# Scores of a half head scaled, masked and minimised by two whole-tile instructions in place of one accumulating instruction per block

## The chip, the cores and the metric

The kernel runs on one core of a Trainium2 chip. The metric is the device time of one execution in microseconds. Three runs of the kernel before gave 688.06, 691.05 and 696.49 us. The engines are TensorE (PE, with its weight loads as PEld), VectorE (DVE), ScalarE (ACT), GpSimd (POOL) and SyncE (SP, which issues DMAs).

## What is computed

Three layers follow each other on 4 sequences of 576 tokens. The change lies in the first.

```python
scores = scale * q @ k.T                 # 4 x 8 heads, 576 x 576, head_dim 64, scale 1/8
rel = pos[:, None] - pos[None, :]
mask_plain = (rel >= 0) & (rel < 32)                       # heads 0 to 3
mask_dil = (rel >= 0) & (rel < 128) & (rel % 4 == 0)       # heads 4 to 7
scores = where(mask, scores, -1e9)
attn = exp(scores - max(scores)); attn /= sum(attn) + 1e-9
x = attn @ v
```

The second layer routes each token to one of 8 experts (relu(x w1[e]) w2[e], times a probability) by a gate that can keep the expert of the token before; the third is a gated unit with a spatial product over the 576 tokens (relu(x w_in), normalised half, mixed over tokens, gate, w_out).

## The kernel before, in words

**Attention** (`attention`, line 583) goes through 64 half heads: 16 pairs of heads (4 sequences x 4 pairs), each with two halves and two heads. A sequence's pairs 0 and 1 are "plain" heads: a half is 3 blocks of 96 queries against 128 keys. Pairs 2 and 3 are dilated heads, handled by residue modulo 4: a half is 4 blocks of 72 queries against 72 keys (first half) or 104 keys (second half). `geom` (line 722) gives these sizes. So 32 half heads have 3 blocks of 96x128, 16 have 4 of 72x72 and 16 have 4 of 72x104; in their order, 8 plain half heads are followed by 8 dilated ones (72, 72, 104, 104 columns and again).

One half head i passes these steps: `qk` (line 727) multiplies queries and keys into a PSUM tile `S` of [128, 4, 128] (two buffers); `soft` (line 743) on VectorE computes, block by block, (score + mask) x -0.125 into `ms` and the minimum of each row into `mxa` (line 751, one accumulating instruction a block), and POOL then subtracts the minimum (line 754); `expo` (line 759) takes exp(-ms) on ScalarE; `pT` (line 767) transposes on TensorE and evacuates to `ptS`; `pv` (line 778) multiplies with the values on TensorE into a PSUM tile `PV` (two buffers, line 787), then adds 1e-9 to the sums (line 793), takes the reciprocal (line 795) and writes `xo`, the product of both (line 797), the last three on VectorE. Every second half head a finished part of x is transposed, split into a high part `xTh` on ScalarE and a low part `xTl` on VectorE (lines 550 and 551), for the router.

**The order** of every engine's instructions is the order in which the program writes them. The loop at line 877 writes, in turn i: `qk(i)`, `soft(i)`, then what is left of `fill` and of the router's budget, one transposition of later queries or keys, `expo(i-1)`, `pT(i-3)`, the product of `pv(i-4)`, and a transposition of x. The three VectorE steps of `pv` are put between the instructions of `soft` of the next turn: `advance()` writes the next of them, and `feed(i)` writes one step of the router (a small VectorE, ScalarE or PE instruction), while the turn's budget lasts (10 or 5 steps). In the kernel before, `advance()` and `feed(i)` are called behind each block, 3 or 4 times a half head.

`evac` (line 639) sends an evacuation to ScalarE or VectorE, whichever has less in `load_of`; `soft` adds a figure to both at lines 756 and 757. The masks are made at lines 584 to 588 by POOL: `masks[:, 0]` for a first block, `masks[:, 1]` for the others; the fill `MASKED` is added before the scaling, hence -8e9.

After attention come the expert blocks, whose first products begin while attention ends, and the third layer.

Of the kernel before, what the change touches and what calls it, by code (L numbers as in the profile page):

```python
# [10 lines left out]
F32 = mybir.dt.float32  # L11
# [5 lines left out]
ALU = mybir.AluOpType  # L17
AX = mybir.AxisListType
# [43 lines left out]
PTL = 3  # L62
QB, KB = 96, 128
QD, KD = 72, 104
MASKED = -8.0e9
GATE = -1.5 * 2.0 ** -23


# [1 line left out]
def moe_stack(ctx: ExitStack, tc: tile.TileContext, q, k, v, w_gate, w_local, w1, w2, w_in, w_sp, b_sp, w_out, out):  # L70
    nc = tc.nc
# [63 lines left out]
    def steps(f):  # L135

        g = f()
        if g is not None:
            yield from g
# [441 lines left out]
    load_of = {"act": 0.0, "dve": 0.0}  # L581

    def attention(aw, ap, qkp, plan):
        masks = aw.tile([QB, 2, KB], F32, name="masks", bufs=1)
        nc.gpsimd.memset(masks, 0.0)
        for m in range(2):
            for base, cm, st in ((32 * m, 1, -1), (31 - 32 * m, -1, 1)):
                nc.gpsimd.affine_select(out=masks[:, m], in_=masks[:, m], pattern=[[st, KB]], compare_op=ALU.is_ge, fill=MASKED, base=base, channel_multiplier=cm)
        loads, qT, xout = {}, {}, {}
        xTs = {}  # L590

# [130 lines left out]
        def geom(u, half):  # L722
            if u % 4 < 2:
                return QB, KB, 3
            return QD, (QD, KD)[half], 4
# [17 lines left out]
        def soft(i):  # L743
            u, hh, half = hs[i]
            nq, nk, nb = geom(u, half)
            ps = live[i][0]
            ms = aw.tile([96, 4, 128], F32, name="ms", bufs=2)
            mx = aw.tile([96, 4], F32, name="mxa", bufs=3)
            for j in range(nb):
                m = 0 if (half == 0 and (u % 4 >= 2 or j == 0)) else 1  # L750
                nc.vector.tensor_tensor_reduce(out=ms[0:nq, j, 0:nk], in0=ps[0:nq, j, 0:nk], in1=masks[0:nq, m, 0:nk], scale=-0.125, scalar=3.0e38, op0=ALU.add, op1=ALU.min, accum_out=mx[0:nq, j:j + 1])  # L751
                advance()
                feed(i)
            nc.gpsimd.tensor_tensor(out=ms[0:nq, 0:nb, 0:nk], in0=ms[0:nq, 0:nb, 0:nk], in1=mx[0:nq, 0:nb].unsqueeze(2).to_broadcast([nq, nb, nk]), op=ALU.subtract)  # L754
            live[i] += [ms, mx]
            load_of["dve"] += 520 + nb * (70 + nk * 1.04)
            load_of["act"] += 190 + nb * nk * 0.84

        def expo(i):
# [76 lines left out]
        def advance():  # L836
            for _ in range(len(fill)):
                g = fill.popleft()
                if next(g, fill) is not fill:
                    fill.append(g)  # L840
# [6 lines left out]
        name, ends = [None, None], {}  # L847

        def feed(i):

            nonlocal budget
            for n in FIRST:
                while budget > 0:
                    if begun[n] is None:
                        if not queues[n]:
                            break
                        f = queues[n][0]
                        if hasattr(f, "on_pe") and i < ends.get(getattr(f, "needs", None), ended[n]) + GAP:
                            break
                        begun[n], name[n] = steps(queues[n].popleft()), f  # L860
                    cost = next(begun[n], fill)
                    if cost is fill:
                        begun[n], ended[n], ends[name[n]] = None, i, i
                        continue
                    budget -= cost or 1
                    load_of["dve"] += STAGE_COST * (cost or 1)
                    return
# [9 lines left out]
        for i in range(n_hs + LAG + EXTRA):  # L877
# [4 lines left out]
            if i < n_hs:  # L882
                u, hh, half = hs[i]
                if i % 4 == 3 and u >= EU or i % 4 == 0 and u <= EU:
                    w = u + 2 if i % 4 else u + 1
                    if w < npair:
                        urgent.extend(turns(w))
                if i % 4 == 3:
                    if u + 4 < npair:
                        load_qk(u + 4)  # L890
                    if 3 <= u + 2 < npair:
                        load_v(u + 2)
                qk(i)
                if i < 6:
                    heat(HS[i])
                soft(i)
# [11 lines left out]
            if 0 <= i - LAG < n_hs:  # L908
                fill.append(pv(i - LAG))
                advance()  # L910
                u, hh, half = hs[i - LAG]
# [27 lines left out]
    aw = aws.enter_context(tc.tile_pool(name="aw", bufs=2))  # L939
# [166 lines left out]
    ready = {"w1": lambda: state["listed"] > 1, "in": lambda: "idx1" in state}  # L1106
    plan = [(i, ready.get(kind, lambda: True), early(kind, c)) for i, kind, c in PLAN]
    stages = attention(aw, ap, qkp, plan)
    done = {"gather": 2, 1: 2, 2: 2}

# [382 lines left out]
```

## Time and profile before

| what | value |
|---|---|
| median of three runs | 691.05 us |
| the profiled execution | 691.2 us |
| its span, first to last instruction | 689.5 us |
| PE busy | 665.4 us, 97% |
| PEld busy | 572.5 us, 83% |
| DVE busy | 420.9 us, 61% |
| ACT busy | 378.0 us, 55% |
| POOL busy | 122.8 us, 18% |

Busy time of an engine is the time in which at least one of its instructions runs; instructions of one engine can overlap, so that their durations add up to more. "Idle before" is the engine's idle time ahead of an instruction, with what ended it; a wait for several things is put down to the last. Times in a timeline count from the first instruction.

### The profile page before, as it was taken

The numbers are of one execution on the slowest core, as the hardware profiler recorded it, in microseconds if no ns is written. First come the engines' busy times: TensorE is split into PE (matmuls) and PEld (weight loads), VectorE is DVE, ScalarE is ACT, GpSimd is POOL, SyncE is SP. The second block draws the span as 40 slices with busy tenths as digits, with TensorE's granted clock in tenths as the row PEclk, the third lists the DMA queues.
The fourth block names the chain that finished last, engine by engine and source line by source line (L and its number), as shares of the span: only waits on it lengthen the run. The fifth ranks groups of instructions, "written<-read, shape, count | busy, mean of one in ns | idle before, by whom it ended". The sixth has DMA issues, their size and how long they took to land. (4 is left out here: it accounts for less than half of the span.)

```text
span 689.5 us, 14119 instructions
## 1 busy us (share of the span) xinstructions
PE 665.4 (97%) x4393; PEld 572.5 (83%) x4394; DVE 420.9 (61%) x1411; ACT 378.0 (55%) x780; POOL 122.8 (18%) x194
## 2 busy tenths in 40 slices
PE   8899898989999999999999999988999999999998
PEld 6899898886478888888888887867998998998996
DVE  4577969878866747978876856333764164064051
ACT  5688676763635746767665647435725327235322
POOL 6343424441212101101111031002100110000000
PEclk9999999999999999999999999999999999999999
DMA  8876555595445876786565755415100210200102
GB/s 153 173 174 156 120 132 142 148 340 171 154 152 182 299 245 200 284 318 202 221 215 207 290 175 223 154 48 165 47 17 31 68 41 0 77 17 1 61 2 76
DMA packets 98321, 101.34 MB, mean 147 GB/s; under 512 B 59200, under 2 KB 68672, under 8 KB 98240
## 3 DMA queue, kind: packets, MB, share of 16 engines
q1 hardware_dynamic: 94800, 89.10, 42.0%
q0 software_dynamic: 3440, 11.27, 5.0%
q8 instruction: 36, 0.59, 0.3%
q14 instruction: 45, 0.37, 0.2%
HBM read 139.68 MB, written 17.30 MB: 228 GB/s over the span
## 5 line engine op out<-in xcount | busy, mean ns | idle before, releaser
L1045 PE MATMUL yp<-w2h,hh 128*128 128x512 f32 x176 | 70.9, 403 | 0.5 <-ACT hh L1034 0.5
L982 POOL DMA_INDIRECT xs<-x_d,ix x25 | 30.6, 1225 | 225.7 <-DVE ix L980 67.9
L1047 PE MATMUL yp<-w2h,hl 128*128 128x512 f32 x176 | 69.0, 392 | 0.8 <-DVE hl L1035 0.8
L1046 PE MATMUL yp<-w2l,hh 128*128 128x512 f32 x176 | 68.5, 389 | 0.0
L1011 PE MATMUL hp<-w1h,xh 128*128 128x512 f32 x168 | 67.5, 401 | 0.2 <-issue 0.2
L1013 PE MATMUL hp<-w1h,xl 128*128 128x512 f32 x168 | 65.8, 392 | 0.1
L1012 PE MATMUL hp<-w1l,xh 128*128 128x512 f32 x168 | 65.6, 391 | 0.0
L751 DVE CUSTOM_DVE_ANT_0 ms<-S,masks 96x128 f32<-96x128 f32 (+2 forms) x224 | 54.5, 249 | 18.0 <-PE S L740 9.5
L754 POOL TENSOR_TENSOR ms<-ms,mxa 96x384 f32<-96x384 f32 (+2 forms) x64 | 51.1, 798 | 67.2 <-DVE mxa L751 39.4
L551 DVE TENSOR_TENSOR w2l<-raw,w2h 128x1024 fp32r<-128x1024 f32 x40 | 47.7, 1223 | 14.8 <-ACT w2h L550 13.1
L740 PE MATMUL S<-kz,qT 128*96 128x128 f32 (+2 forms) x448 | 54.0, 262 | 0.2 <-POOL kz L602 0.2
L787 PE MATMUL PV<-vt,ptS 128*96 128x65 f32 (+2 forms) x448 | 44.9, 242 | 7.0 <-issue 2.3
L1035 DVE TENSOR_TENSOR hl<-hTp,hh 128x512 fp32r<-128x512 f32 x44 | 30.4, 690 | 33.7 <-ACT hh L1034 33.2
L551 DVE TENSOR_TENSOR w1l<-raw,w1h 128x1024 fp32r<-128x1024 f32 x40 | 46.4, 1223 | 4.1 <-ACT w1h L550 3.3
L787 PEld LDWEIGHTS PV<-vt,ptS 128*96 128x96 f32 (+2 forms) x448 | 39.3, 158 | 9.5 <-issue 3.2
L740 PEld LDWEIGHTS S<-kz,qT 128*72 128x72 f32 (+1 forms) x448 | 46.1, 158 | 0.9 <-POOL kz L602 0.7
L550 ACT ACTIVATE w2h<-raw 128x1024 fp32r<-128x1024 f32 x40 | 41.2, 1060 | 5.0 <-PE yp L1047 3.8
L550 ACT ACTIVATE gtiles<-gt 128x288 fp32r<-128x288 f32 (+2 forms) x48 | 15.7, 359 | 48.3 <-DVE gt L1389 48.3
L1034 ACT ACTIVATE hh<-hTp 128x512 fp32r<-128x512 f32 x44 | 26.2, 596 | 28.4 <-DVE hl L1035 22.9
L1047 PEld LDWEIGHTS yp<-w2h,hl 128*128 128x128 f32 x176 | 33.0, 188 | 9.0 <-DVE hl L1035 1.9
L550 ACT ACTIVATE w1h<-raw 128x1024 fp32r<-128x1024 f32 x40 | 39.3, 1048 | 2.1 <-ACT w1h L550 0.9
L765 ACT ACTIVATE pp<-ms 96x384 f32<-96x384 f32 (+2 forms) x64 | 32.2, 504 | 12.0 <-POOL ms L754 11.4
(310 smaller groups left out, 1725.1 us busy)
## 6 DMA issues: line engine op xcount, KB each, us to landing
raw<-in_moe_w SPq DMA_DIRECT2D x188, 512.0 KB
y_d<-y SPq DMA_DIRECT2D x30, 256.0 KB
qk<-in_q SPq DMA_DIRECT2D x32, 144.0 KB
qk<-in_k SPq DMA_DIRECT2D x32, 144.0 KB
x_d<-xo SPq DMA_DIRECT2D x32, 144.0 KB
scratch<-in_moe_w_in SPq DMA_DIRECT2D x8, 512.0 KB
out<-o SPq DMA_DIRECT2D x15, 256.0 KB
vt<-in_v SPq DMA_DIRECT2D x48, 64.0 KB
```

What stands on the lines that cost most here:

```text
L550: nc.scalar.activation(dst_h, src, AF.Copy)
L551: (eng or nc.vector).tensor_tensor(out=dst_l, in0=src, in1=dst_h.bitcast(F32), op=ALU.subtract)
L740: nc.tensor.matmul(ps[0:nq, j, 0:nk], l, r, start=True, stop=True)
L751: nc.vector.tensor_tensor_reduce(out=ms[0:nq, j, 0:nk], in0=ps[0:nq, j, 0:nk], in1=masks[0:nq, m, 0:nk], scale=-0.125, scalar=3.0e38, op0= ...
L754: nc.gpsimd.tensor_tensor(out=ms[0:nq, 0:nb, 0:nk], in0=ms[0:nq, 0:nb, 0:nk], in1=mx[0:nq, 0:nb].unsqueeze(2).to_broadcast([nq, nb, nk]), ...
L787: nc.tensor.matmul(ops[0:nq, j], ptS[0:nk, j, 0:nq], r, start=True, stop=True)
L1011: nc.tensor.matmul(ps[n], xh[:, kk], wh[:, kk, cs], start=(kk == 0), stop=False)
L1012: nc.tensor.matmul(ps[n], xh[:, kk], wl[:, kk, cs], start=False, stop=False)
L1013: nc.tensor.matmul(ps[n], xl[:, kk], wh[:, kk, cs], start=False, stop=(kk == 3))
L1045: nc.tensor.matmul(ps, hh[:, f], P["w2h"][:, f], start=(f == 0), stop=False)
L1046: nc.tensor.matmul(ps, hh[:, f], P["w2l"][:, f], start=False, stop=False)
L1047: nc.tensor.matmul(ps, hl[:, f], P["w2h"][:, f], start=False, stop=(f == 7))
```

## The change

The mask tile has four planes (the last two are copies of the second), its fill is 1e9, added after the scaling. Per half head, one scalar_tensor_tensor over all 3 or 4 blocks computes score x -0.125 + mask, and one tensor_reduce takes the minimum of each block's rows. Two calls each of `advance()` and `feed(i)` lie between the two and two behind them, 4 in every half head. The load figure for VectorE is another.

```diff
@@ -62,7 +62,7 @@
 PTL = 3
 QB, KB = 96, 128
 QD, KD = 72, 104
-MASKED = -8.0e9
+MASKED = 1.0e9
 GATE = -1.5 * 2.0 ** -23
 
 
@@ -581,11 +581,12 @@
     load_of = {"act": 0.0, "dve": 0.0}
 
     def attention(aw, ap, qkp, plan):
-        masks = aw.tile([QB, 2, KB], F32, name="masks", bufs=1)
-        nc.gpsimd.memset(masks, 0.0)
+        masks = aw.tile([QB, 4, KB], F32, name="masks", bufs=1)
+        nc.gpsimd.memset(masks[:, 0:2], 0.0)
         for m in range(2):
             for base, cm, st in ((32 * m, 1, -1), (31 - 32 * m, -1, 1)):
                 nc.gpsimd.affine_select(out=masks[:, m], in_=masks[:, m], pattern=[[st, KB]], compare_op=ALU.is_ge, fill=MASKED, base=base, channel_multiplier=cm)
+        nc.vector.tensor_copy(masks[:, 2:4], masks[:, 1:2].to_broadcast([QB, 2, KB]))
         loads, qT, xout = {}, {}, {}
         xTs = {}
 
@@ -746,14 +747,23 @@
             ps = live[i][0]
             ms = aw.tile([96, 4, 128], F32, name="ms", bufs=2)
             mx = aw.tile([96, 4], F32, name="mxa", bufs=3)
-            for j in range(nb):
-                m = 0 if (half == 0 and (u % 4 >= 2 or j == 0)) else 1
-                nc.vector.tensor_tensor_reduce(out=ms[0:nq, j, 0:nk], in0=ps[0:nq, j, 0:nk], in1=masks[0:nq, m, 0:nk], scale=-0.125, scalar=3.0e38, op0=ALU.add, op1=ALU.min, accum_out=mx[0:nq, j:j + 1])
-                advance()
-                feed(i)
+            if u % 4 < 2:
+                mk = masks[0:nq, half:half + nb, 0:nk]
+            else:
+                mk = masks[0:nq, half:half + 1, 0:nk].to_broadcast([nq, nb, nk])
+            nc.vector.scalar_tensor_tensor(out=ms[0:nq, 0:nb, 0:nk], in0=ps[0:nq, 0:nb, 0:nk], scalar=-0.125, in1=mk, op0=ALU.mult, op1=ALU.add)
+            advance()
+            feed(i)
+            advance()
+            feed(i)
+            nc.vector.tensor_reduce(mx[0:nq, 0:nb], ms[0:nq, 0:nb, 0:nk], axis=AX.X, op=ALU.min)
+            advance()
+            feed(i)
+            advance()
+            feed(i)
             nc.gpsimd.tensor_tensor(out=ms[0:nq, 0:nb, 0:nk], in0=ms[0:nq, 0:nb, 0:nk], in1=mx[0:nq, 0:nb].unsqueeze(2).to_broadcast([nq, nb, nk]), op=ALU.subtract)
             live[i] += [ms, mx]
-            load_of["dve"] += 520 + nb * (70 + nk * 1.04)
+            load_of["dve"] += 640 + nb * nk * 2.08
             load_of["act"] += 190 + nb * nk * 0.84
 
         def expo(i):
```

## Rows read from the trace of the kernel before

**Rows 1.** Section 1 of the page: busy us (share of the span), instructions.

```profile
PE 665.4 (97%) x4393; PEld 572.5 (83%) x4394; DVE 420.9 (61%) x1411; ACT 378.0 (55%) x780; POOL 122.8 (18%) x194
```

**Rows 2.** Busy time by stretches: from:to, length, engines' busy time (instructions), granted clock, DMA.

```profile
40.40:64.60 24.20, 23.61 (x278) 22.55 (x276) 17.03 (x121) 19.71 (x50) 10.03 (x17) 1.00 0.69 158
64.60:84.40 19.80, 17.13 (x198) 16.06 (x198) 18.40 (x112) 14.46 (x38) 9.17 (x16) 0.96 0.54 130
...
104.20:133.70 29.50, 26.10 (x299) 23.94 (x298) 27.94 (x172) 21.27 (x53) 13.08 (x23) 1.00 0.54 130
...
144.60:156.70 12.10, 10.23 (x106) 9.56 (x104) 10.14 (x67) 6.88 (x17) 4.33 (x7) 0.86 1.05 354
...
200.00:420.00 220.00, 220.00 (x1079) 183.30 (x1078) 156.66 (x237) 135.06 (x195) 29.45 (x32) 1.00 0.68 242
```

**Rows 3.** Waits of PE, 40 to 160 us: us in total, times, longest.

```profile
PE PV L787 <- DVE xo L797: 1.4, 3, 0.8
```

**Rows 4.** Groups by form, line 751, VectorE: count, busy us, mean ns, idle before.

```profile
L751 DVE CUSTOM_DVE_ANT_0 ms<-S,masks 96x128 f32<-96x128 f32 x96 | 25.5, 273 | 7.8 <-PE S L740 4.4 <-ACT pp L765 3.2
...
L751 DVE CUSTOM_DVE_ANT_0 ms<-S,masks 72x104 f32<-72x104 f32 x64 | 15.9, 248 | 3.1 <-PE S L740 3.0
L751 DVE CUSTOM_DVE_ANT_0 ms<-S,masks 72x72 f32<-72x72 f32 x64 | 13.7, 215 | 7.1 <-ACT ls L163 3.9 <-PE S L740 2.1 <-PE R L468 0.9
```

**Rows 5.** Timeline of VectorE, one plain half head: start us, length us.

```profile
43.33 0.28 DVE L751 CUSTOM_DVE_ANT_0 ms<-S,masks 96x128 f32<-96x128 f32 x1
43.54 0.08 DVE L751 DVE_READ_ACCUMULATOR2_ANT mxa<- 96x1 f32 x1
...
43.91 0.25 DVE L751 CUSTOM_DVE_ANT_0 ms<-S,masks 96x128 f32<-96x128 f32 x1
...
44.09 0.41 DVE L797 TENSOR_TENSOR xo<-PV,rc 72x256 f32<-72x256 f32 x1
```

**Rows 6.** Timeline of VectorE, end of a 72x72 half head and a 72x104 one.

```profile
36.41 0.22 DVE L751 CUSTOM_DVE_ANT_0 ms<-S,masks 72x72 f32<-72x72 f32 x1
36.56 0.08 DVE L751 DVE_READ_ACCUMULATOR2_ANT mxa<- 72x1 f32 x1
36.68 0.26 DVE L751 CUSTOM_DVE_ANT_0 ms<-S,masks 72x104 f32<-72x104 f32 x1
36.87 0.08 DVE L751 DVE_READ_ACCUMULATOR2_ANT mxa<- 72x1 f32 x1
...
37.22 0.23 DVE L751 CUSTOM_DVE_ANT_0 ms<-S,masks 72x104 f32<-72x104 f32 x1
...
37.38 0.42 DVE L797 TENSOR_TENSOR xo<-PV,rc 72x256 f32<-72x256 f32 x1
```

**Rows 7.** Timeline of VectorE, three scalar_tensor_tensor; the third reads what the second writes.

```profile
259.40 0.69 DVE L1081 SCALAR_TENSOR_TENSOR scratch<-scratch 128x512 f32<-128x512 uint32 x1
260.01 0.69 DVE L1082 SCALAR_TENSOR_TENSOR scratch<-scratch 128x512 int32<-128x512 int32 x1
260.73 0.69 DVE L1083 SCALAR_TENSOR_TENSOR scratch<-scratch 128x512 f32<-128x512 f32 x1
```

**Rows 8.** Line 487, the widest reduce: ns min/median/max, starts, forms.

```profile
L487 DVE TENSOR_REDUCE pv<-pm x1: 903/903/903, 217.9 to 217.9; 128x90 f32<-128x720 f32 x1
```

**Rows 9.** Timeline, two places: an xo and the second product that follows it.

```profile
32.35 0.35 DVE L797 TENSOR_TENSOR xo<-PV,rc 96x192 f32<-96x192 f32 x1
...
32.85 0.31 PE L787 MATMUL PV<-vt,ptS 72*72 72x65 f32 x2
...
90.75 0.35 DVE L797 TENSOR_TENSOR xo<-PV,rc 96x192 f32<-96x192 f32 x1
...
91.32 0.47 PE L787 MATMUL PV<-vt,ptS 128*96 128x65 f32 x3
```

**Rows 10.** Timeline, start: POOL's masks and VectorE's first copy of scores' operands.

```profile
3.84 1.25 POOL L588 TENSOR_SCALAR_AFFINE_SELECT masks<-masks 96x128 f32<-96x128 f32 x4
...
6.39 0.45 DVE L645 COPY kz<-T 64x288 f32<-64x288 f32 x1 [2.11 <-PE T L670]
```

## The prediction, made before the change was run

> **What bounds the kernel now.** I read the page first: TensorE is busy for 97% of the span and VectorE for 61% [rows 1], so extra VectorE work should cost nothing on the average, and the question is where it is not average. Next I read busy time by stretches, cut at the starts of half heads. Attention, where the edited instructions run, ends near 157 us. In 40.4:64.6 VectorE is busy for 17.03 of 24.20 us and TensorE for 23.61: TensorE sets the pace. In 64.6:84.4, 104.2:133.7 and 144.6:156.7, where the router's small VectorE steps fall, VectorE is busy for 18.40 of 19.80, 27.94 of 29.50 and 10.14 of 12.10 us, and TensorE loses 2.67, 3.40 and 1.87 us. In 200:420 TensorE is busy for all of 220.00 us [rows 2]; so a microsecond lost in attention is not won back there. The waits of TensorE between 40 and 160 us then name what it lacks: the second product (L787) waits on VectorE's `xo` (L797), which frees its PSUM buffer [rows 3]. The chain that ended last covers only the tail of the program and doesn't help.
>
> **What goes.** 64 half heads lose their 224 accumulating instructions, each with an accumulator read, on a form 96x128 (32 half heads of 3), 72x104 (16 of 4) and 72x72 (16 of 4) [rows 4]. Their durations, 273, 248 and 215 ns, are not what they cost: VectorE starts the next instruction before the last has ended. The timeline shows 0.21 us from a 96x128 to what follows (43.33 to 43.54), the second the same, and 0.18 for the third (43.91 to 44.09): 0.60 us a half head [rows 5]. For 72x104 it is 0.19, 0.18, 0.16 and 0.18 (first and third shown), together 0.71 us; for 72x72 0.15, 0.15, 0.12 and 0.15, together 0.57 us [rows 6]. The accumulator read takes no slot of its own: what follows starts at the same moment. So 32 x 0.60 + 16 x 0.71 + 16 x 0.57 = 39.7 us of VectorE's time go.
>
> **What comes.** One scalar_tensor_tensor and one reduce per half head, over 384, 416 or 288 columns. The same kind of scalar_tensor_tensor over 512 columns lets its successor start after 0.61 us (259.40 to 260.01) and lasts 0.69 [rows 7]; at 0.96 GHz 512 columns are 0.533 us, so 0.08 us is fixed: 0.475, 0.51 and 0.375 us. The reduce of 720 columns lasts 903 ns [rows 8], that is 0.153 + 720 x 1.042 ns; with the same 0.08 us of overlap it blocks VectorE for 0.47, 0.50 and 0.37 us. Together 0.945, 1.01 and 0.745 us, and 32 x 0.945 + 16 x 1.01 + 16 x 0.745 = 58.3 us. Difference a half head: +0.345, +0.30, +0.175 us; in all +18.6 us of VectorE. The cause is plain: each column now passes VectorE twice.
>
> [...]
>
> **What moves.** The reciprocal now follows the add that feeds it directly when no router step lies between. A dependent successor starts 0.72 us after an instruction that lasts 0.69 [rows 7], so the add (0.15 us long, 0.07 of slot) holds it to 0.18 us. `xo` then starts 0.475 + 0.18 + 0.09 + 0.47 = 1.215 us after the half head's first instruction instead of 0.76 [rows 5], 0.455 later; 0.58 later for 72x104 (0.70 now [rows 6]) and 0.43 for 72x72 (0.59).
>
> **On the path: the saturated stretches.** 64.6:84.4 holds 3 plain half heads, 3 of 72x104 and 2 of 72x72: 1.04 + 0.90 + 0.35 = 2.3 us more; 104.2:133.7 holds 7, 3 and 2: 3.7 us; 144.6:156.7 holds 0, 3 and 2: 1.25 us. VectorE's idle time there is 1.40, 1.56 and 1.96 us [rows 2]. If it takes up all it can, 0.9 + 2.1 + 0 = 3.0 us reach TensorE; if none, because VectorE idles while it waits for ScalarE and those waits move along, 7.2 us. I take 4.5: part of the idle time is such waiting, and a stretch may hand some lag on to the easier one behind it.
>
> **On the path: elsewhere.** VectorE has room, but `xo` comes later, and in seven places outside those stretches a second product starts at most 0.50 us after the end of `xo`; the first at 32.85 (`xo` ends 32.70), the last at 91.32 (`xo` ends 91.10) [rows 9]. About 0.08 us between the two is the hand-over. Growth by 0.43 to 0.58 us less the margins of 0.02 to 0.42 gives 0.51, 0.13, 0.16, 0.44, 0.28, 0.44 and 0.32: 2.3 us. Zero if a stall at one place gives the next its margin back; I take 1.5.
>
> **At nothing.** The copy of the mask (96x256) waits for POOL's mask, done at 5.09 us, on a VectorE that then stands idle until 6.39 [rows 10]; without that cover it would cost 0.35 us. The scores' bank comes free earlier, but no wait of TensorE is put on it, so no gain. The minimum is complete some 0.3 us later in plain half heads (1.215 + 0.08 behind the first instruction, against 0.58 + 0.25 + 0.08 + hand-over [rows 5]) and about as early as now in the others; the exponential is used two half heads later, which hides it: between -1 and +1 us in all, taken as 0. The raised load figure of line 756 can only move evacuations from VectorE to ScalarE, which spares VectorE a little; also 0.
>
> **Sum.** The profiled execution took 691.2 us (span 689.5): 691.2 + 4.5 + 1.5 = 697.2. The median of the three runs shown, 691.05, is 0.15 lower, so I predict 697.0. A measurement of this kernel tells about 2% (14 us) from no change, so this would be within it.
>
> **Rivals.** Absorbed: TensorE is the bound, S and PV are double-buffered, VectorE's lag is used up in the stretches between; 691 to 692. For it: 23.61 of 24.20 us in 40.4:64.6 [rows 2]. Against it: TensorE's direct waits on `xo`. Chance 0.22.
>
> Faster, because fewer instructions: if VectorE worked them off end to end, a half head would cost 3 x (273 + 80) = 1.06, 4 x (248 + 80) = 1.31 and 4 x (215 + 80) = 1.18 us now [rows 4, 5], and 1.11, 1.18 and 0.91 by the full durations of rows 7 and 8 after: +0.05, -0.13, -0.27. The three stretches would gain 0.8 + 0.5 + 0.9 us, and the time be 689. It decides at whether a successor waits for the accumulator read, and the starts say that it doesn't [rows 5, 6]. Chance 0.06. [...]
>
> [...] Chance 0.12, half of it over 2%.
>
> That the compiler splits the new instructions back into blocks, and the time stays: 0.02.
>
> **How the numbers follow.** Forecast (694 to 701) 0.58. The range 690 to 703 leaves out most of the gain and the far end of the clock case. Slower by over 2%: 0.06 of the clock case and 0.01 else, 0.07; faster by over 2% would need more than half of all TensorE's idle time, 0.02; within 2%: 0.91.
>
> **What would show it.** Right: 64 scalar_tensor_tensor near 560, 593 and 460 ns and 64 reduces near 553, 587 and 454; VectorE's busy time up by some 15 us; `xo` 1.1 to 1.3 us behind its half head's first instruction; longer waits of L787 on L797; TensorE busier by nothing and idle longer in the three stretches. Wrong: a reduce well under 400 ns, unchanged waits on `xo`, or a shorter time to the start of the first expert block.

## The result and the profile after

The changed kernel took 698.86 us (median of 4 runs, 698.29 to 701.07), the kernel before 690.63 in the same comparison (4 runs, 688.06 to 696.49): a ratio of 1.0125, 95% interval 1.0094 to 1.0157, slower by some 8 us. In a second comparison (9 runs against 19) it took 697.61 against 690.63: 1.0097, 1.0062 to 1.0131. The profiled execution shown here is the longest of the first four, 701.07 us, so the single trace overstates the difference. The profiled execution of the kernel before took 691.2 us.

Section 1 of the page of the changed kernel, for [rows 1]:

```profile
PE 670.8 (96%) x4393; PEld 575.9 (82%) x4394; DVE 440.5 (63%) x1088; ACT 380.0 (54%) x784; POOL 123.5 (18%) x194
```

VectorE has 323 instructions fewer and is busy 19.6 us longer (440.5 - 420.9). The fewer instructions do more work.

Busy time by stretches of the changed kernel, with the columns of [rows 2]. The first six follow each other and are cut at the same half heads as the rows of before; the last lies in the expert blocks:

```profile
41.40:67.50 26.10, 24.08 (x277) 22.77 (x277) 20.53 (x71) 19.98 (x51) 9.76 (x17) 1.00 0.62 141
67.50:88.80 21.30, 17.59 (x196) 15.81 (x195) 20.82 (x69) 14.25 (x37) 9.33 (x16) 0.96 0.52 121
88.80:111.80 23.00, 22.63 (x210) 21.33 (x209) 15.29 (x55) 14.20 (x37) 6.67 (x14) 0.82 0.49 110
111.80:143.70 31.90, 26.02 (x296) 23.75 (x295) 31.13 (x115) 21.28 (x53) 13.04 (x23) 1.00 0.50 126
143.70:154.80 11.10, 11.10 (x127) 10.11 (x127) 8.64 (x37) 7.43 (x22) 5.03 (x10) 1.00 1.02 298
154.80:167.00 12.20, 9.74 (x96) 9.12 (x94) 10.92 (x34) 6.76 (x16) 4.30 (x6) 0.86 1.04 378
210.00:430.00 220.00, 220.00 (x1079) 183.25 (x1078) 156.96 (x237) 135.23 (x195) 30.24 (x32) 1.00 0.69 242
```

The third and the fifth of these stretches were, in the kernel before:

```profile
84.40:104.20 19.80, 19.47 (x207) 18.30 (x207) 12.47 (x94) 13.80 (x37) 6.74 (x13) 0.95 0.58 130
...
133.70:144.60 10.90, 10.79 (x124) 9.81 (x123) 6.88 (x58) 7.49 (x22) 5.06 (x10) 1.00 0.97 305
```

Compare the lengths, the first number behind each window, with [rows 2] and these two. Up to the first cut 1.0 us is added (41.4 for 40.4), then 1.9, 1.5, 3.2, 2.4, 0.2 and 0.1 us: 10.3, against 9.8 between the two spans (699.3 - 689.5). The three saturated stretches grew by 1.5, 2.4 and 0.1 us: 4.0. In two of them VectorE was already busy for 93 and 95% of the time; now it is for 20.82 of 21.30 and 31.13 of 31.90, and TensorE idles longer there, 3.7 and 5.9 us for 2.67 and 3.40. The third, 88.8:111.8, is of another kind: VectorE is busy for 15.29 of 23.00 us, TensorE for 22.63. Its granted clock is 0.82 for 0.95. A time x (1 - clock) of 23.0 x 0.18 = 4.1 for 19.8 x 0.05 = 1.0 us: 3.1 of its growth of 3.2 us go with the lower granted clock (six matmuls of line 741 last 0.84 us in this trace at 1.00, from 86.25, and 1.54 at 0.50, from 89.36). In the expert blocks TensorE is busy for all of 220.00 us in both, and of the 10.3 us all but 0.5 are still there at the end.

The changed kernel cut finer around the fall:

```profile
83.50:85.90 2.40, 0.93 (x11) 0.78 (x12) 2.40 (x7) 2.33 (x8) 2.21 (x5) 1.00 0.64 136
85.90:87.00 1.10, 1.10 (x16) 1.10 (x14) 1.10 (x7) 1.05 (x4) 0.68 (x1) 1.00 0.04 11
87.10:97.10 10.00, 9.69 (x58) 9.13 (x58) 6.72 (x21) 4.17 (x10) 2.59 (x4) 0.50 0.54 121
```

Ahead of the fall TensorE was busy for only 0.93 of 2.40 us, while VectorE was busy for all of them, and then for 1.10 of 1.10; at 0.50 it was busy for 9.69 of the 10.00 us (58 matmul records). The kernel before has a fall in the same place, and it is shorter:

```profile
83.10:86.30 3.20, 3.20 (x23) 3.20 (x21) 2.07 (x11) 1.78 (x5) 1.75 (x3) 0.50 0.40 92
```

This is also most of the reason why TensorE is *busier* by 5.4 us with the same 4393 instructions: 22.63 for 19.47 in this stretch.

The new groups by form, up to 185 us, for [rows 4] (count, busy us, mean ns, idle before):

```profile
L754 DVE SCALAR_TENSOR_TENSOR ms<-S,masks 96x384 f32<-96x384 f32 x32 | 17.5, 546 | 6.0 <-PE S L741 4.7 <-ACT pp L775 1.1
L759 DVE TENSOR_REDUCE mxa<-ms 96x3 f32<-96x384 f32 x32 | 16.9, 528 | 0.2
L754 DVE SCALAR_TENSOR_TENSOR ms<-S,masks 72x416 f32<-72x416 f32 x16 | 9.3, 578 | 2.8 <-PE S L741 2.8
L759 DVE TENSOR_REDUCE mxa<-ms 72x4 f32<-72x416 f32 x16 | 8.9, 558 | 0.0
L754 DVE SCALAR_TENSOR_TENSOR ms<-S,masks 72x288 f32<-72x288 f32 x16 | 7.2, 447 | 4.7 <-ACT ls L163 3.1 <-PE S L741 1.5
L759 DVE TENSOR_REDUCE mxa<-ms 72x4 f32<-72x288 f32 x16 | 6.7, 422 | 0.0
```

And the half head of [rows 5] in the changed kernel's timeline:

```profile
44.24 0.55 DVE L754 SCALAR_TENSOR_TENSOR ms<-S,masks 96x384 f32<-96x384 f32 x1
44.70 0.15 DVE L803 TENSOR_SCALAR rc<-PV 72x4 f32<-72x4 f32 x1
44.88 0.17 DVE L805 RECIPROCAL rc<-rc 72x4 f32<-72x4 f32 x1
44.98 0.52 DVE L759 TENSOR_REDUCE mxa<-ms 96x3 f32<-96x384 f32 x1
45.42 0.41 DVE L807 TENSOR_TENSOR xo<-PV,rc 72x256 f32<-72x256 f32 x1
45.75 0.54 DVE L754 SCALAR_TENSOR_TENSOR ms<-S,masks 96x384 f32<-96x384 f32 x1
```

The same half head of the kernel before ([rows 5], from 43.33) ends where the next one begins:

```profile
44.43 0.27 DVE L751 CUSTOM_DVE_ANT_0 ms<-S,masks 96x128 f32<-96x128 f32 x1
```

Read the first column, not the second. From this half head's first instruction to the next one's VectorE takes 45.75 - 44.24 = 1.51 us, for 44.43 - 43.33 = 1.10 before. The steps of the 1.51: 0.46 us to the add, 0.18 to the reciprocal that needs it, 0.10 to the reduce, 0.44 for the reduce, 0.33 for `xo`. `xo` starts 1.18 us behind the half head's first instruction (0.76 before). The half head's last minimum is complete at 44.98 + 0.52 = 45.50, 1.26 us behind that start; before it was 44.17 - 43.33 = 0.84 (the accumulator read behind line 751 at 44.09, 0.08 long). So two results come later: `xo`, which TensorE waits for, and the minimum, which POOL waits for.

TensorE's waits of the changed kernel from 40 to 170 us (us in total, times, longest), for [rows 3]:

```profile
PE PV L797 <- DVE xo L807: 3.2, 5, 1.3
PE PV L797 <- ACT ptS L643: 2.0, 3, 1.0
```

The wait on `xo` grew from 1.4 to 3.2 us. POOL's wait for the minimum, between 20 us and the end of attention, was in the kernel before

```profile
POOL ms L754 <- DVE mxa L751: 34.1, 31, 2.6
```

and is in the changed one

```profile
POOL ms L764 <- DVE mxa L759: 58.5, 37, 4.0
```

POOL has room (18% busy), so this is no cost yet; it becomes one where ScalarE's exponential, next in the chain, waits for POOL.

### The profile page after: what moved, and what is told of

The parts are those of the page before. It is cut to its first block, busy times and chain, and to the rows that moved or that the text cites. A ratio compares the mean times of both kernels' runs of the same rounds, so it can differ in the third digit from the quotient of the medians.

```text
span 699.3 us, 13798 instructions
## 1 busy us (share of the span) xinstructions
PE 670.8 (96%) x4393; PEld 575.9 (82%) x4394; DVE 440.5 (63%) x1088; ACT 380.0 (54%) x784; POOL 123.5 (18%) x194
## 3 DMA queue, kind: packets, MB, share of 16 engines
q1 hardware_dynamic: 94800, 89.10, 41.4%
## 5 line engine op out<-in xcount | busy, mean ns | idle before, releaser
L754 DVE SCALAR_TENSOR_TENSOR ms<-S,masks 96x384 f32<-96x384 f32 (+2 forms) x64 | 33.9, 529 | 13.5 <-PE S L741 9.1
L775 ACT ACTIVATE pp<-ms 96x384 f32<-96x384 f32 (+2 forms) x64 | 32.3, 504 | 14.8 <-POOL ms L764 14.4
```

## The experiments

Three theories were on the table. *Occupancy*: VectorE's added time costs where VectorE is nearly full, wherever it is put. *Late xo*: TensorE waits for the PSUM buffer. *Late minimum*: the path from the minimum over POOL to the exponential and the evacuations behind it on ScalarE.

Each kernel's runs spread by some 3 to 9 us, and the granted clock goes with it: over 160 runs, compared within their own kernel, the time moves by 0.70 us for each us of span x (1 - mean granted clock). So beside each ratio I give the difference of the mean times and the part of it by which this clock figure differs ("clock"); the rest is an estimate of what the edit does at full clock. At 0.70 us per us it takes off somewhat too much, so both stand in the table behind the experiments. All ratios are against the kernel before.

**The form in the dilated half heads alone, and in the plain ones alone.** The condition was added to `soft`, with extra mask planes, since the two forms need different fills:

```diff
-            for j in range(nb):
...
+            if u % 4 < 2:
+                for j in range(nb):
...
+            else:
+                mk = masks[0:nq, 2 + half:3 + half, 0:nk].to_broadcast([nq, nb, nk])
...
+                nc.vector.tensor_reduce(mx[0:nq, 0:nb], ms[0:nq, 0:nb, 0:nk], axis=AX.X, op=ALU.min)
```

The other kernel has the two branches exchanged.

> The two-instruction form in the 32 dilated half heads alone, the plain ones as before. Theory (the loss is made in plain half heads, whose xo comes 0.45 us later and whose VectorE work grows by 0.345 us; the traces show the starts of the dilated groups drift by 0.3 to 0.6 us a group): 1 to 3 us above the kernel before. Rival (each microsecond of added VectorE work costs the same wherever it stands; 7.6 of 18.6 us are added here): 3.4 us above. Rival (load figures and moved evacuations): nothing.

> The two-instruction form in the 32 plain half heads alone. Theory: 5.5 to 7.5 us above the kernel before, nearly all of the change's 8.2. Rival (same price everywhere, 11.0 of 18.6 us): 4.8 us above.

Measured: dilated alone 693.74 us, 1.0038 (1.0021 to 1.0056); plain alone 695.83, 1.0060 (1.0038 to 1.0083). By the prediction's slots the dilated half heads add 16 x 0.30 + 16 x 0.175 = 7.6 us of VectorE and the plain ones 32 x 0.345 = 11.0; they cost 2.8 and 4.5 us of mean time, 0.37 and 0.41 us per us. The two parts add up to 7.3, against 7.4 for the whole change. Both shapes pay about alike, as an occupancy price would; the theory on record for the plain ones (5.5 to 7.5 us) missed, and its rival's 3.4 and 4.8 us lie nearer. For `xo` this doesn't yet tell occupancy from lateness, which grow together. For the minimum it does: in the dilated half heads it isn't late. With a fourth block, `xo` stands ahead of that block in the kernel before, and the last minimum is read behind it. One half head of 72x104 from 36.68 [rows 6], its last read:

```profile
37.89 0.08 DVE L751 DVE_READ_ACCUMULATOR2_ANT mxa<- 72x1 f32 x1
```

and the same half head in the changed kernel:

```profile
37.34 0.58 DVE L754 SCALAR_TENSOR_TENSOR ms<-S,masks 72x416 f32<-72x416 f32 x1
38.12 0.55 DVE L759 TENSOR_REDUCE mxa<-ms 72x4 f32<-72x416 f32 x1
```

The minimum is complete 37.97 - 36.68 = 1.29 us behind the first instruction before, 38.67 - 37.34 = 1.33 after. Compared half head by half head in the traces, dilated alone has it 0.04 us later for 72x104 and 0.19 earlier for 72x72 (medians of 16); plain alone has it 0.41 later in the plain half heads (median of 32). So dilated alone paid 2.8 us without a later minimum.

**The product before the minimum.** Three of the four `advance`/`feed` pairs stand ahead of the reduce, so that `xo` leaves before it and the minimum later:

```diff
-            nc.vector.tensor_reduce(mx[0:nq, 0:nb], ms[0:nq, 0:nb, 0:nk], axis=AX.X, op=ALU.min)
             advance()
             feed(i)
+            nc.vector.tensor_reduce(mx[0:nq, 0:nb], ms[0:nq, 0:nb, 0:nk], axis=AX.X, op=ALU.min)
```

> The changed kernel with the three steps that end in xo ahead of the reduce, so that xo starts about 0.85 us behind the first instruction in place of 1.2. If lateness of xo is the price: 3 to 5 us above the kernel before instead of 8.2. If occupancy of VectorE alone is the price: 8 to 9 us above, since the dependent steps now stand side by side and the minimum comes 0.4 us later.

Measured: 702.72 us, 1.0172 (1.0146 to 1.0198), slower than the change itself. If late `xo` were the main cost, this would have won it back. The waits of TensorE from 40 to 170 us in this kernel:

```profile
PE PT L783 <- ACT ptS L643: 3.7, 9, 0.6
...
PE PV L797 <- DVE xo L807: 1.1, 2, 0.5
```

The wait on `xo` did fall, from 3.2 to 1.1 us, below that of the kernel before. In its place the transposition of the probabilities waits for ScalarE's evacuation, nine times. And ScalarE waits for POOL; from 20 to 170 us:

```profile
ACT pp L775 <- POOL ms L764: 23.2, 32, 1.8
```

In the changed kernel that row is

```profile
ACT pp L775 <- POOL ms L764: 14.4, 21, 1.7
```

So the stall moved from one result to the other. But VectorE's own time grew as well. The half head of 44.24 above, here from 44.32 to the next one's first instruction:

```profile
44.32 0.54 DVE L754 SCALAR_TENSOR_TENSOR ms<-S,masks 96x384 f32<-96x384 f32 x1
...
45.52 0.54 DVE L761 TENSOR_REDUCE mxa<-ms 96x3 f32<-96x384 f32 x1
45.98 0.55 DVE L754 SCALAR_TENSOR_TENSOR ms<-S,masks 96x384 f32<-96x384 f32 x1
```

That is 1.66 us for 1.51: add, reciprocal and `xo` stand side by side, and the last two each wait for the one that feeds them. The minimum is complete 46.06 - 44.32 = 1.74 us behind the first instruction (1.26 in the changed kernel). The run therefore doesn't part a later minimum from an engine held longer.

**The load figure put back.**

```diff
-            load_of["dve"] += 640 + nb * nk * 2.08
+            load_of["dve"] += 520 + nb * (70 + nk * 1.04)
```

> The changed kernel with the load figure of before, so that evacuations are shared out as before. Theory: as the changed kernel, 8 us above the kernel before, within 1 us. Rival (evacuations moved to ScalarE cost something): 2 us or more less than the changed kernel.

Measured: 700.06 us, 1.0119 (1.0095 to 1.0144), as the changed kernel. The evacuations' placement isn't the cause.

**A useless add on VectorE in the kernel before**, of 96x256 elements, in the 32 plain half heads. It was put in three places: behind the half head's blocks, between the last accumulating instruction and `xo`, and ahead of the first block. Once two were put behind:

```diff
+        dmy = aw.tile([QB, 6, KB], F32, name="dmy", bufs=1)
+        nc.vector.memset(dmy, 0.0)
...
+            if u % 4 < 2:
+                nc.vector.tensor_tensor(out=dmy[:, 0:2], in0=dmy[:, 2:4], in1=dmy[:, 4:6], op=ALU.add)
```

Behind the blocks it delays neither result of its own half head:

> The kernel before, with one useless VectorE addition of 96x256 (about 0.345 us of slot) behind the accumulating instructions and xo of each plain half head: the change's added occupancy without its later xo. If lateness of xo is the price: 0 to 2 us above the kernel before. If occupancy is the price: 4 to 6 us above.

Ahead of the blocks it delays both the minimum and `xo`:

> The same addition ahead of the accumulating instructions: the same occupancy, and xo 0.345 us later. If lateness of xo is the price: 4 to 6 us above the kernel before, and 3 us or more above the addition behind. If occupancy is the price: 4 to 6 us above, as behind.

Between them it delays `xo` alone:

> The kernel before with the same useless addition as in the two runs with one, now between the last accumulating instruction and xo of each plain half head: the minimum is on time, xo is 0.345 us late. Behind xo it cost 2.8 us, ahead of all 6.8. If late xo is what makes that difference: 6 to 7.5 us above the kernel before. If the late minimum makes it: 2 to 4 us above. Apart from the clock (span times one minus the mean granted clock taken off) all three places should lie within 1 us, 4 to 5 us above.

Two behind:

> Two such additions behind xo in each plain half head, 22 us of VectorE in all. If VectorE's room is used up after the first: 9 to 13 us above the kernel before, more than twice the single one's 2.8, and 0.6 us or more per added us for the second dose. If VectorE's work stays mostly hidden: 5 to 6 us above.

Measured: behind 692.86 us, 1.0040 (1.0018 to 1.0063); between 692.35, 1.0023 (0.9996 to 1.0049), no difference that can be told; ahead 696.98, 1.0098 (1.0072 to 1.0123); two behind 703.73, 1.0193 (1.0149 to 1.0238). `xo` later by one add costs no more than the same add where `xo` isn't late: for the plain half heads no price of its own can be seen, though the interval (up to 3.4 us) leaves room for a small one. The two adds don't hold VectorE alike: the ones behind made it 16.1 us busier, the ones between 9.3 (see the last section); per added us both cost about as much, 0.17 and 0.18 us. The add ahead of the blocks, with the minimum late too, costs 7.1 - 1.6 = 5.5 us more than the one between; 2.4 with the clock taken off. (It also frees the scores' bank later, which these two don't part.) ScalarE's waits for POOL from 20 to 170 us, with the add between:

```profile
ACT pp L769 <- POOL ms L758: 12.2, 19, 1.8
```

and with the add ahead:

```profile
ACT pp L769 <- POOL ms L758: 16.0, 24, 1.5
```

for 11.4 in the kernel before. They don't follow the time, though. With the add behind, at 692.86 us, the wait is as long as with the add ahead:

```profile
ACT pp L769 <- POOL ms L758: 15.8, 23, 1.9
```

Two adds behind, 42.8 us of added durations in all, are dear without any lateness of the minimum or of `xo` in their own half head: occupancy has a price. The single one behind, 20.0 us of durations, cost 2.8; the second added 11.0. With the clock taken off it is 4.3 and 6.7, for 16.1 and 20.8 us of added busy time: 0.27 and 0.32 us per us, so most of the rise goes with the clock. With these adds POOL's subtraction of a plain half head also takes longer (983 and 985 ns on the mean, 824 before), and ScalarE waits 23.3 us for POOL with two; so the path over POOL isn't untouched there.

**The minimum before the product.** One pair ahead of the reduce, three behind it:

```diff
+            nc.vector.tensor_reduce(mx[0:nq, 0:nb], ms[0:nq, 0:nb, 0:nk], axis=AX.X, op=ALU.min)
             advance()
             feed(i)
-            nc.vector.tensor_reduce(mx[0:nq, 0:nb], ms[0:nq, 0:nb, 0:nk], axis=AX.X, op=ALU.min)
```

> The changed kernel with one step instead of two between the two instructions: the add alone stands there, and reciprocal and xo follow the reduce. VectorE's work is the same; the minimum is complete about 0.2 us earlier (1.1 us behind the first instruction) and xo starts about 0.1 us earlier, since the reciprocal no longer waits for the add. Occupancy theory: as the changed kernel, within 1 us. If the lateness of the minimum (by POOL, the exponential and what stands behind it on ScalarE) has a price: 2 to 4 us below the changed kernel.

Measured: 700.90 us (695.46 to 704.61), 1.0122 (1.0067 to 1.0178). No gain in time, and the widest scatter of all. With the clock taken off it stands at 4.9 us, where the change has 6.7 and 5.1 (with the old load figure): at most a small gain. The minimum is indeed earlier, 45.01 - 43.89 = 1.12 us behind the first instruction for 1.26, and ScalarE waits less for POOL than even in the kernel before. But here too VectorE takes longer for the half head, 1.58 us for 1.51, against what was expected ("VectorE's work is the same"):

```profile
43.89 0.54 DVE L754 SCALAR_TENSOR_TENSOR ms<-S,masks 96x384 f32<-96x384 f32 x1
...
44.46 0.55 DVE L757 TENSOR_REDUCE mxa<-ms 96x3 f32<-96x384 f32 x1
...
45.47 0.54 DVE L754 SCALAR_TENSOR_TENSOR ms<-S,masks 96x384 f32<-96x384 f32 x1
```

```profile
ACT pp L775 <- POOL ms L764: 9.5, 15, 1.3
```

This run does not show a price of the late minimum.

**A step less on VectorE.** The 1e-9 added to the sums changes nothing in float32, since each row's sum holds the 1 of its own minimum. It was left out of the changed kernel, and of the kernel before:

```diff
-            nc.vector.tensor_scalar_add(rc[0:nq, 0:nb], ops[0:nq, 0:nb, 64], 1e-9)
-            yield
-            nc.vector.reciprocal(rc[0:nq, 0:nb], rc[0:nq, 0:nb])
+            nc.vector.reciprocal(rc[0:nq, 0:nb], ops[0:nq, 0:nb, 64])
```

> The changed kernel without the addition of 1e-9 to the row sums, which are at least 1 (one exponential is exp(0)), so that fp32 does not change: the reciprocal reads PSUM itself. xo starts about 0.18 us earlier and VectorE spends 0.07 us less a half head. If lateness of xo is the price: 2.5 to 4 us below the changed kernel. If occupancy: 1 to 2 us below.

> The kernel before without that addition: xo about 0.07 to 0.1 us earlier, 0.07 us less VectorE a half head. Both theories: 0.5 to 2 us below the kernel before; more if several second products still stand directly behind xo.

Measured: changed 695.49 us, 1.0085 (1.0058 to 1.0112); before 688.51, 0.9978 (0.9961 to 0.9995). The change costs 5.3 + 2.0 = 7.3 us with this step gone from both, as with it. This does not clear the held step. The half head of 44.24, here from 44.68:

```profile
44.68 0.55 DVE L754 SCALAR_TENSOR_TENSOR ms<-S,masks 96x384 f32<-96x384 f32 x1
45.15 0.17 DVE L803 RECIPROCAL rc<-PV 72x4 f32<-72x4 f32 x1
45.35 0.42 DVE L805 TENSOR_TENSOR xo<-PV,rc 72x256 f32<-72x256 f32 x1
45.70 0.54 DVE L759 TENSOR_REDUCE mxa<-ms 96x3 f32<-96x384 f32 x1
```

With one step fewer, `xo` comes ahead of the reduce. It starts 0.20 us behind the reciprocal that feeds it, where the independent reduce started 0.10 behind (44.88 to 44.98): the hold is still there, at another step. The minimum is complete 46.24 - 44.68 = 1.56 us behind the first instruction, later than in the changed kernel (1.26), and yet the kernel costs 5.3 us where the change costs 7.4. It also has less VectorE work. The second of the two is faster than both kernels of this case, by little. Its one wait on `xo` from 40 to 170 us:

```profile
PE PV L787 <- DVE xo L795: 0.2, 1, 0.2
```

**The changed kernel again**, beside the add between, the two behind and the early minimum:

> The changed kernel once more, on the chip of the three runs beside it, for more runs of its time and granted clock: 7 to 9.5 us above the kernel before; mean granted clock 0.987 to 0.990 against 0.992 to 0.993, which by itself is 2 to 4 us.

Measured: 697.61 us, 1.0097 (1.0062 to 1.0131).

Differences of the mean times to the kernel before, in us; the last column is VectorE's busy time in the profiled execution less the 420.9 us of the kernel before:

| kernel | difference | clock | rest | VectorE |
|---|---|---|---|---|
| dilated alone | 2.8 | -0.2 | 3.0 | 9.0 |
| plain alone | 4.5 | -0.8 | 5.3 | 11.1 |
| product before the minimum | 11.5 | 3.7 | 7.7 | 20.2 |
| old load figure | 8.7 | 3.6 | 5.1 | 21.1 |
| add behind | 2.8 | -1.5 | 4.3 | 16.1 |
| add between | 1.6 | -1.0 | 2.6 | 9.3 |
| add ahead | 7.1 | 2.1 | 5.0 | 12.6 |
| two adds behind | 13.8 | 2.8 | 11.0 | 36.9 |
| minimum before the product | 9.9 | 5.0 | 4.9 | 21.7 |
| changed, without 1e-9 | 5.3 | 1.0 | 4.4 | 14.4 |
| before, without 1e-9 | -2.0 | -1.2 | -0.9 | -4.8 |
| changed again | 7.4 | 0.7 | 6.7 | 19.6 |

In every kernel that adds work the rest is 0.23 to 0.48 us for each us by which VectorE is busier, wherever the work stands and whichever of the two results is late; for the change it is 6.7 / 19.6 = 0.34. (With the product put first, the plain half head shown takes 0.15 us longer than the change's, 4.8 us over 32 of them, and VectorE's busy time is only 0.6 us higher; so the last column may understate that kernel.) Occupancy is what these kernels have in common. The differences between them (add ahead 0.40, add between 0.28) leave room for a smaller part that depends on the place.

## Why the prediction was right, and where not

The forecast of 697.0 was 0.6 below the median of the second comparison and 1.9 below the first; the direction held, and so did the first of its two mechanisms, VectorE's added time in the stretches where VectorE has no room. The second, a price of the later `xo`, did not.

**Slots.** Two passes in place of one: predicted +18.6 us of VectorE, measured +19.6 of busy time (the list of signs had some 15). In part this is luck. In the half head shown above the two passes take 0.46 + 0.44 = 0.90 us, less than the 0.945 of the sum; the held reciprocal takes 0.18 - 0.07 = 0.11 more than the add's slot, which the prediction counted for `xo` but not for VectorE. Together the half head grew by 0.41 us, not by 0.345. The rate behind the prediction's slots, 0.96 columns a ns or 1.042 ns a column, is that of line 751 in [rows 4]: 24 columns more (104 to 128) take 273 - 248 = 25 ns more; in the changed kernel 128 columns more (288 to 416) take 578 - 447 = 131 ns for line 754 and 558 - 422 = 136 for line 759. Predicted durations 560, 593 and 460 ns for line 754 and 553, 587 and 454 for line 759; the groups above show 546, 578, 447 and 528, 558, 422, all 2 to 7% lower. `xo` was to come 1.215 us behind the first instruction; 1.18 here. That starts, not durations, count was the choice that mattered, and it brought down the rival of fewer instructions (689): the 224 instructions that went gave back less than the 128 that came took. The compiler's split didn't occur (64 and 64 instructions).

**Saturated stretches.** Predicted 4.5 us out of bounds of 3.0 and 7.2; the traces show 4.0. 64.6:84.4 gave 1.5 and 104.2:133.7 gave 2.4; 144.6:156.7 only 0.1, because VectorE's idle time there took up the 0.8 us that were added (10.92 for 10.14).

**Absorbed.** The rival's 691 to 692 fell. The adds show what there is to it: one of them between, with slots of some 11 us in all, cost 1.6, so most of it was indeed hidden; two behind cost 13.8.

**Elsewhere, the step whose reason failed.** The prediction put 1.5 us down to `xo` coming later outside the saturated stretches. The traces show 3.1 us there without the stretch of the clock (1.0 + 1.9 + 0.2), and the reason is not borne out. The hand-over from `xo` to the product, taken as some 0.08 us, is 0.05 to 0.06 at the three waits of [rows 3] (68.56 to 68.61, 108.10 to 108.16, 133.20 to 133.25). The add between makes `xo` 0.34 us later in the plain half heads (medians; 0.41 in the change) and cost 1.6 us, no more per us of VectorE's time than the one behind. In the changed kernel without the 1e-9, `xo` is early and TensorE waits on it for only 0.3 us between 40 and 170 us, yet the kernel costs 5.3. What the runs show in its place is a price for VectorE's added time as such, about a third of it at full clock; by which wait it reaches TensorE outside the saturated stretches stays open.

**"Between -1 and +1 us in all, taken as 0", the later minimum.** The prediction expected some 0.3 us in the plain half heads and none in the others. It came to 0.42 and to none: for the kernel before it had added 0.58 + 0.25 + 0.08, where the row of the read gives 44.17 - 43.33 = 0.84. Whether the lateness has a price stays open. For it speaks the add ahead against the add between: 5.5 us more, 2.4 with the clock taken off. The product put first costs 4.1 us more than the change (1.0 with the clock taken off), but VectorE takes 0.15 us longer for a plain half head there. Against it speak three runs. Dilated alone paid 2.8 us without a later minimum. Without the 1e-9 the minimum of the changed kernel is later still, and the kernel is cheaper by 2.1 us. The early minimum won nothing that can be told, though VectorE takes 0.07 us longer there. So no part of the change's own 7.4 us is shown to be the minimum's, and none is ruled out.

**Clock.** The clock case had a chance of 0.12, half of it over 2%. No run of the change shows a loss of that size: it stood at 1.0125 and 1.0097. What came was a longer fall of the granted clock, 10.00 us at 0.50 in the place of 3.20, worth some 3 us in that execution, and with it most of the 5.4 us by which TensorE was busier, where "by nothing" was forecast. Over the sets of runs the clock's share is 0.7 us for the change and 3.6 for the change with the old load figure. What makes one fall longer than another wasn't tried by itself.

**Evacuations and the mask copy at nothing.** The old load figure changed nothing; the copy wasn't tried alone, but all that happens before 41.4 us, it included, cost 1.0.

## What to carry to other kernels

Price an instruction by the distance between its start and the next one's start. Here three accumulating instructions with their minima took 0.60 us; the whole-tile instruction without them took 0.46, and the reduction as an instruction of its own another 0.44, a whole second pass over the columns. Price it in the order in which it will stand, too: in these traces an instruction directly behind the add (0.15 us long) or the reciprocal (0.17) that feeds it started 0.18 or 0.20 us later, an independent one 0.07 to 0.10 later. For the same reason, when you reorder instructions to test a wait, check that the engine's own time per round stayed the same; in two of the runs above it did not, and they settle less than they seem to. The result with the visible wait (`xo`) was not shown to cost anything by itself. And on this kernel, in which TensorE is busy for 97% of the span, extra work on VectorE was hidden to some three fifths (7.4 us for 18.6), not altogether.

## What the hardware did unexpectedly

The useless add lasts 0.42 us, but about 1.06 where POOL's subtraction has just begun. In the kernel with the add behind, timeline (start, length):

```profile
17.34 0.82 POOL L758 TENSOR_TENSOR ms<-ms,mxa 96x384 f32<-96x384 f32 x1 [1.58 <-DVE mxa L753]
17.38 1.06 DVE L757 TENSOR_TENSOR dmy<-dmy 96x256 f32<-96x256 f32 x1
```

The add's end, 18.44, lies 0.28 us behind POOL's, 18.16. With the add between, VectorE begins first, and the add lasts 0.42 us:

```profile
44.44 0.42 DVE L755 TENSOR_TENSOR dmy<-dmy 96x256 f32<-96x256 f32 x1
...
44.66 0.88 POOL L758 TENSOR_TENSOR ms<-ms,mxa 96x384 f32<-96x384 f32 x1 [2.10 <-DVE mxa L753]
```

All 32 adds of each kernel (shortest, median, longest in ns), first behind:

```profile
L757 DVE TENSOR_TENSOR dmy<-dmy x32: 403/418/1084, 8.7 to 138.5; 96x256 f32<-96x256 f32 x32
```

then between:

```profile
L755 DVE TENSOR_TENSOR dmy<-dmy x32: 406/416/431, 9.2 to 135.1; 96x256 f32<-96x256 f32 x32
```

The adds behind last 20.0 us in all, the adds between 13.3. So the former take 6.7 us longer for the same work, which is why their cost is not read from their durations; that all of it goes with POOL's subtractions is the author's estimate from the two places shown. The change's own instructions show no such case: the longest of line 754 lasts 589 ns and the longest of line 759 571, for means of 578 and 558 in the widest form.

The second surprise was how much of the spread between runs of one kernel goes with the granted clock: 0.70 us of time per us of that figure, over 160 runs. In the second comparison, the kernel before took 696.22 us at a mean clock of 0.983 and 687.03 at 0.997.
